# Half-width transposes for q and k, and a rearranged first batch, in an attention kernel followed by a token-mixing block

## The chip, the core and the metric

The kernel runs on one core of a Trainium2 chip. Five engines run their own instruction lists: TensorE (PE; its weight loads are shown as PEld), VectorE (DVE), ScalarE (ACT), GpSimd (POOL) and SyncE (SP). They wait for each other by semaphores. The metric is the device time of one execution in microseconds; the kernel before has a median of 174.81 us over 10 runs (174.43 to 175.35).

## The reference

Four batches, 8 heads, 768 tokens, head size 64. Attention with 8 global keys, a causal window of 96 and a bias that falls linearly with distance; then a token-mixing block on the 512 channels:

```python
scores = scale * q @ k^T
keep   = (key < 8) | (0 <= query - key < 96)
dist   = where(global and not local, 96, |query - key|)
a      = softmax(where(keep, scores - slope[h] * dist, -1e9))
x      = (a @ v) as (batch, 768, 512)
theta  = x @ w_theta
y      = w_tok_r @ (x * cos(theta)) + w_tok_i @ (x * sin(theta))
u      = x + y
out    = u + max(u @ w_ch, 0)
```

## The kernel before

The 768 tokens make 6 tiles of 128, the 8 heads make 4 pairs. A tile of keys meets only its own tile of queries, the next one, and the 8 global keys, so the scores of a pair are 11 blocks of 128x128 for each head, in three chunks of 4, 4 and 3 (`score_mms`, L279). The two heads of a pair lie on 64 partitions each, and their score matmuls use the upper and the lower half of TensorE's rows (form 64*128 in the profile). ACT takes the exponential of a chunk (`score_exp`, L298). In batch 0 the bias is added beforehand by a matmul of a diagonal matrix with the distances (`score_bias`, L270, on `diag` and `dist`); in the other batches the exponential is multiplied by a table `etab` (L312, L315), which `bias_table` (L140) makes on ACT. `values` (L336) multiplies by v, with a column of ones for the row sums, and DVE divides (L360, L362). `xtrans` (L364) turns the result into `xT`: by TensorE and a copy in batch 0, by DMA otherwise. Then `theta` (L378), cosine and sine on ACT (L395), products on DVE (L398), `mix` (L403), `utrans` (L418), `chan` (L430).

For the scores q and k must lie with the head size on the partitions. They are loaded with tokens on the partitions. Batch 0, pair 0 comes as float32 in `qk32` by SP and ACT (L99); the other loads convert to bf16 and are issued by POOL (L73, L82). DVE (for pair 0, DVE and ACT) copies a pair so that the two heads of a token tile are 128 adjacent columns: `qkn`, in `cast0` (L193) for batch 0 and in `prep_copy` (L224) for batches 1 and 2. Then one transpose for each token tile, 6 for q and 6 for k (L204, L244), writes a tile in PSUM, which DVE and ACT copy to `qT` and `kT` (L211, L249, L251). `kglob` (L214) copies four key blocks to `kG` and puts the global keys over their first 8 columns. Batch 3 is turned by DMA (`prep_dma`, L256) and has no `qkn`.

Order of the work: batch 0 up to `theta` and the tables is written out by hand (L510 to L574); each engine's list is kept in that order. After that a scheduler places the instructions, guided by the order of the program and by anchors (`behind`). `weave` (L488) mixes two lists of steps by their weights: the main one, token mixing of batch b, and the side one, the preparations and the attention of batch b + 1. `prep` of batch 1 is in the side list of batch 0, beginning when 0.3 of the main weight is done; `prep` of batch 2 is in that list too, among the attention of batch 1. The buffers of q and k serve two batches: batch 3 is loaded where batch 1 was, so its loads (L82) wait until that is read. PSUM is handed out as two double-width tiles (`ps_big`) and four single ones (`ps_small`), in rotation.

By hand, batch 0 is a loop over pairs. Each turn of the loop takes the exponentials, copies out the next pair's transposes, does the values of the pair before, and casts the pair after next; that pair's transposes are issued after the next pair's second chunk of scores. The last pair's values follow the loop (L566), then the first weight transposes, `xtrans` of the last pair, and `theta`.

Of the kernel before, what the change touches and what calls it, by code (L numbers as in the profile page):

```python
# [9 lines left out]
FP = mybir.dt.float32  # L10
BF = mybir.dt.bfloat16
AF = mybir.ActivationFunctionType
# [4 lines left out]
def kernel(  # L17
# [13 lines left out]
    nc = tc.nc  # L31
    B, H, S, D = q.shape
    T = 128
    NT = S // T
    DM = H * D
    NC = DM // T
    NP = H // 2
    NG = int(n_global)
    NL = int(n_local)
    W = T + NL  # L40
    scale = 1.0 / math.sqrt(D)
    slopes = [2.0 ** (-8.0 * (h + 1) / H) for h in range(H)]
# [91 lines left out]
    def diagonals(p):  # L134
        for h in (2 * p, 2 * p + 1):
            nc.vector.tensor_scalar(diag[:, h], ident, -slopes[h] / scale, None, op0=ALU.mult)

    etab = const.tile([T, H, 5, T], BF)

    def bias_table(p):  # L140
        for h in (2 * p, 2 * p + 1):
            nc.scalar.activation(etab[:, h], dist[:, 0:5], AF.Exp, scale=-slopes[h])

    halfpi = const.tile([T, 1], FP)
    junk = const.tile([T, 1], FP)
# [41 lines left out]
    def behind(eng):  # L187

        return tc.issue_after(anchor[eng]) if eng in anchor else nullcontext()

    tiles0 = {}

    def cast0(p, i_, eng, h=None):  # L193
        if (p, "n") not in tiles0:
            tiles0[p, "n"] = att.tile([T, NT, 2, 2, D], BF, name="qkn", bufs=2)
        src = qk32[:, i_] if p == 0 else loads[0][0][:, i_, 2 * p:2 * p + 2]
        hs = slice(0, 2) if h is None else slice(h, h + 1)
        eng(out=tiles0[p, "n"][:, :, i_, hs].rearrange("p t h d -> p h t d"), in_=src[:, hs])

    def turn0(p, i_):  # L200
        qkn = tiles0[p, "n"]
        ps = tiles0[p, i_] = ps_small([T, NT, T], BF)
        for t_ in range(NT):
            nc.tensor.transpose(ps[:, t_, :], qkn[:, t_, i_].rearrange("p h d -> p (h d)"), ident)  # L204

    def out0(p, i_, copy, half=None):
        to = qkT.setdefault((0, p), [None, None, None])
        if to[i_] is None:
            to[i_] = att.tile([T, S], BF, name=("qT", "kT")[i_], tag=("qT", "kT")[i_], bufs=6)
        ns = slice(0, T) if half is None else slice(half * T // 2, (half + 1) * T // 2)  # L210
        copy(out=to[i_].rearrange("p (n t) -> p n t", t=NT)[:, ns],  # L211
             in_=tiles0[p, i_].rearrange("p t n -> p n t")[:, ns])

    def kglob(b, p):  # L214
        kT = qkT[(b, p)][1]
        kG = qkT[(b, p)][2] = att.tile([T, NT - 2, T], BF, name="kG", bufs=6)
        with behind("dve") if b == B - 1 else nullcontext():
            nc.vector.tensor_copy(
                out=kG, in_=kT[:, T:(NT - 1) * T].rearrange("p (t n) -> p t n", t=NT - 2))
            nc.vector.tensor_copy(out=kG[:, :, 0:NG], in_=kT[:, None, 0:NG].to_broadcast([T, NT - 2, NG]))  # L220

    qkns = {}

    def prep_copy(b, p):  # L224
        qk = loads[b][0]
        qkn = qkns[b, p] = att.tile([T, NT, 2, 2, D], BF, name="qkn", bufs=2)
        with behind("dve"):
            for i_ in range(2):
                nc.vector.tensor_copy(
                    out=qkn[:, :, i_].rearrange("p t h d -> p h t d"), in_=qk[:, i_, 2 * p:2 * p + 2])  # L230

    def prep(b, p):
        if p == 0:
            prep_copy(b, 0)
        if p + 1 < NP:
            prep_copy(b, p + 1)
        qkn = qkns[b, p]
        qT = att.tile([T, S], BF, name="qT", bufs=6)
        kT = att.tile([T, S], BF, name="kT", bufs=6)
        for i_, dst in ((0, qT), (1, kT)):  # L240
            ps = ps_small([T, NT, T], BF)
            with behind("pe"):
                for t_ in range(NT):
                    nc.tensor.transpose(ps[:, t_, :], qkn[:, t_, i_].rearrange("p h d -> p (h d)"), ident)  # L244

            dst = dst.rearrange("p (n t) -> p n t", t=NT)
            src = ps.rearrange("p t n -> p n t")
            if i_ == 0:
                nc.vector.tensor_copy(out=dst, in_=src)  # L249
            else:  # L250
                nc.scalar.copy(out=dst, in_=src)  # L251

        qkT[(b, p)] = [qT, kT, None]
        kglob(b, p)
# [15 lines left out]
    def score_bias(p, c):  # L270
        pb = pbs[0, p, c] = ps_big()
        n = min(4, 2 * NT - 1 - 4 * c)
        s0 = 2 if c else 0
        for hh in range(2):
            nc.tensor.matmul(pb[:, hh, 0:n * T], lhsT=diag[:, 2 * p + hh],
                             rhs=dist[:, s0:s0 + n].rearrange("p s n -> p (s n)"),
                             start=True, stop=False)
# [55 lines left out]
            nc.vector.tensor_copy(out=vG[:, hs], in_=vn[:, hs, 1:NT - 1, :])  # L333
        nc.vector.tensor_copy(out=vG[0:NG, hs], in_=vn[0:NG, hs, 0:1, :].to_broadcast([NG, n, NT - 2, D + 1]))

    def values(b, p, hh):  # L336
        vn = loads[b][1]
        e_t, vG = ebuf[(b, p)], vGs[b]
        h = 2 * p + hh
        if b == 0:  # L340
            po = ps_small([T, 1, 512], FP)
        else:
            if hh == 0:
                pos[(b, p)] = ps_big()
            po = pos[(b, p)][:, hh:hh + 1, :]
        for it in range(NT):
            mms = [(e_t[:, hh, it, 0, :], vn[:, h, it, :])]
            if it:
                mms.append((e_t[:, hh, it - 1, 1, :], vG[:, h, it - 2, :] if it > 1 else vn[:, h, 0, :]))
            o = po[:, 0, it * (D + 1):(it + 1) * (D + 1)]  # L350
            for i_, (l_, r_) in enumerate(mms):
                nc.tensor.matmul(o, lhsT=l_, rhs=r_, start=(i_ == 0), stop=(i_ == len(mms) - 1))  # L352
        if b and hh == 0:
            return
        if b:
            po = pos[(b, p)]
        h0, n = (hh, 1) if b == 0 else (0, 2)
        po4 = po[:, :, 0:NT * (D + 1)].rearrange("p a (t d) -> p a t d", d=D + 1)
        rec = att.tile([T, n, NT, 1], FP, name="rec", tag=f"rec{n}")
        nc.vector.reciprocal(rec, po4[:, :, :, D:D + 1])  # L360
        xv = x_sb[b][:, p, :, h0 * D:(h0 + n) * D].rearrange("p t (a d) -> p a t d", a=n)
        nc.vector.tensor_mul(xv, po4[:, :, :, 0:D], rec.to_broadcast([T, n, NT, D]))  # L362

    def xtrans(b, p, copy=nc.vector.tensor_copy):  # L364
        if b:
            anchor["sp"] = nc.sync.dma_start_transpose(
                out=xT_sb[b][:, p, :].rearrange("p (t s) -> p t s", t=NT),
                in_=x_sb[b][:, p].rearrange("p t d -> p (t d)")).ins
            return
        ps = ps_small([T, S], BF)  # L370
        for st in range(NT):
            nc.tensor.transpose(ps[:, st * T:(st + 1) * T], x_sb[b][:, p, st, :], ident)
        copy(out=xT_sb[b][:, p, :], in_=ps)


    zri, u_sb, uTs, pss, css = {}, {}, {}, {}, {}
# [133 lines left out]
    warm(6)  # L510
    distances()
    diagonals(0)
    cast0(0, 1, dve, 0)
    cast0(0, 1, act, 1)
    turn0(0, 1)
    cast0(0, 0, dve, 0)
    cast0(0, 0, act, 1)
    turn0(0, 0)
    out0(0, 1, act, 0)
    out0(0, 1, dve, 1)  # L520
    out0(0, 0, act, 1)
    out0(0, 0, dve, 0)
    kglob(0, 0)
    score_bias(0, 0)
    score_bias(0, 1)
    score_mms(0, 0, 0)
    score_mms(0, 0, 1)
    score_exp(0, 0, 0)
    cast0(1, 1, dve)
    cast0(1, 0, dve)  # L530
    diagonals(1)
    turn0(1, 1)
    turn0(1, 0)
    for p in range(NP):
        nxt = p + 1 < NP
        score_exp(0, p, 1)
        if nxt:
            out0(p + 1, 1, act)
            out0(p + 1, 0, dve)
            kglob(0, p + 1)  # L540
        if p:
            values(0, p - 1, 0)
            values(0, p - 1, 1)
        score_bias(p, 2)
        score_mms(0, p, 2)
        score_exp(0, p, 2)
        if p + 2 < NP:
            cast0(p + 2, 1, dve)
            cast0(p + 2, 0, dve)
            diagonals(p + 2)  # L550
        if p == 0:
            vglob(0, 0, 4)
        if p == 1:
            vglob(0, 4, 4)
        if nxt:
            score_bias(p + 1, 0)
            score_mms(0, p + 1, 0)
            score_exp(0, p + 1, 0)
            score_bias(p + 1, 1)
            score_mms(0, p + 1, 1)  # L560
            if p + 2 < NP:
                turn0(p + 2, 1)
                turn0(p + 2, 0)
        if p:
            xtrans(0, p - 1, act if p == NP - 1 else dve)
    values(0, NP - 1, 0)  # L566
    values(0, NP - 1, 1)
    trans_w(0, nc.scalar.copy)
    xtrans(0, NP - 1)
    for c in range(NT // 2):  # L570
        theta(0, c, 0)
        theta(0, c, 1)
    for p in range(NP):
        bias_table(p)  # L574
    manual.close()
    for eng in (mybir.EngineType.PE, mybir.EngineType.DVE, mybir.EngineType.Activation):
        last = [i for i in nc.cur_bb.bb.instructions if i.engine == eng][-1]
# [82 lines left out]
```

The softmax here doesn't subtract the row's maximum and nothing guards it: scores larger than these inputs give would overflow.

## Time and profile before

| what | us |
|---|---|
| median of 10 runs | 174.81 |
| the profiled execution | 175.47 |
| its span, first to last instruction | 173.5 |
| PE, DVE, ACT busy in it | 161.0, 128.0, 99.2 |
| copies to `qkn`, batches 1 and 2 (L229, 16) | 5.1 |
| casts to `qkn`, batch 0, pairs 1 to 3 (L198 on DVE, 6) | 2.3 |
| transposes of q and k (L244 96, L204 48), PE busy | 7.6 and 4.0 |
| first exponential starts | 9.32 |
| first `theta` matmul of batch 0 | 27.49 |

How to read it: busy time of an engine is the union of its instructions' times. A matmul is shown with its whole passage (0.22 us for 128 columns), while the next can start long before it ends, so the distance between starts tells what PE spends on one. In a timeline row the first number is the start, the second the length, "x6" says that so many instructions were merged, and what stands in brackets is the idle time before it and what ended it. The granted TensorE clock was 0.996 of full speed.

### The profile page before, as it was taken

How to read it: one execution, taken by the hardware profiler on the slowest of the kernel's cores; microseconds unless marked ns; L12 is line 12 of the kernel's file. 1: busy time of each engine (PE TensorE's matmuls, PEld its weight loads, DVE VectorE, ACT ScalarE, POOL GpSimd, SP SyncE). 2: the span in 40 equal slices, each digit the busy share in tenths (PEclk: the TensorE clock that was granted, in tenths of full speed). 3: DMA queues.
4: the chain of work that ended last, by engine and by line, in shares of the span. 5: the costliest groups of instructions: out<-in, count | busy, mean ns of one | idle time of the engine just before them, and what ended most of it. 6: DMA issues, size and time to landing. Idle time of an engine off the chain costs nothing.

```text
span 173.5 us, 3652 instructions
## 1 busy us (share of the span) xinstructions
PE 161.0 (93%) x1482; PEld 84.3 (49%) x1482; DVE 128.0 (74%) x288; ACT 99.2 (57%) x124; POOL 37.4 (22%) x45
## 2 busy tenths in 40 slices
PE   6689989997999999999999998999999989999991
PEld 1445564453756466544454463444454634444440
DVE  7579964876999999999587588596786837723443
ACT  2489686997587695489834550879347308500010
POOL 8974347004182010099100000000000000000000
PEclk9999999999999999999999999999999999999998
DMA  4999999999999999799999697688137471413335
GB/s 153 186 194 179 210 211 205 205 204 168 164 204 171 162 154 160 95 112 158 211 133 125 156 137 165 140 154 237 31 76 117 122 168 36 155 36 101 105 93 181
DMA packets 75088, 25.92 MB, mean 149 GB/s; under 512 B 63168, under 2 KB 72128, under 8 KB 75072
## 3 DMA queue, kind: packets, MB, share of 16 engines
q0 software_dynamic: 45680, 12.45, 79.0%
q1 hardware_dynamic: 28976, 12.72, 35.0%
q10 hardware_dynamic: 416, 0.52, 0.9%
q8 instruction: 11, 0.18, 0.4%
q14 instruction: 5, 0.04, 0.1%
HBM read 25.69 MB, written 6.29 MB: 184 GB/s over the span
## 4 chain that ended last, share of the span: by engine, by line
PE 50%; DMA 33%; DVE 7%; POOL 5%; issue 1%; ACT 1%; SPq 0%; DVEq 0%; POOLq 0%
PE ps L409 26%; DMA qk<-in_k_dram 11%; PE ps L434 10%; DMA w_nat<-in_moe_w_tok_r_dram 8%; DMA xT<-x_sb 7%; DMA uT<-u 5%; PE pb L295 4%; PE pb L389 3%; PE pb L352 3%; POOL qk L73 3%; PE ps L389 2%; POOL vn L88 2%; DMA kT<-qk 2%; DVE qT L249 1%; DVE zri L398 1%
## 5 line engine op out<-in xcount | busy, mean ns | idle before, releaser
L409 PE MATMUL ps<-zri,w_tokT 128*128 128x512 bf16 x288 | 70.6, 380 | 0.3 <-DVE o_sb L440 0.2
L302 ACT ACTIVATE e<-pb 128x1024 bf16<-128x1024 f32 (+1 forms) x48 | 43.6, 958 | 22.3 <-PE pb L295 22.1
L409 PEld LDWEIGHTS <-w_tokT 128*128 128x128 bf16 x288 | 26.1, 98 | 28.9 <-issue 1.0
L414 DVE TENSOR_TENSOR u<-x_sb,ps 128x512 bf16<-128x512 bf16 x24 | 16.4, 682 | 14.6 <-PE ps L409 14.6
L434 PE MATMUL ps<-w_ch_bf,uT 128*128 128x512 bf16 x96 | 24.2, 380 | 0.4 <-DMA uT<-u 0.4
L398 DVE TENSOR_TENSOR zri<-x_sb,cs 128x512 bf16<-128x512 bf16 x48 | 17.9, 418 | 7.8 <-ACT cs L395 7.5
L440 DVE SCALAR_TENSOR_TENSOR o_sb<-ps,u 128x512 f32<-128x512 f32 (+1 forms) x25 | 16.5, 663 | 3.3 <-PE ps L434 3.3
L395 ACT ACTIVATE cs<-pb,halfpi 128x1024 bf16<-128x1024 f32 x8 | 8.9, 1115 | 15.6 <-PE pb L389 15.6
L312 DVE TENSOR_TENSOR e<-e,etab 128x1024 bf16<-128x1024 bf16 (+1 forms) x24 | 14.7, 615 | 3.7 <-ACT e L302 3.7
L389 PE MATMUL pb<-w_theta_bf,xT 128*128 128x512 bf16 x64 | 15.1, 380 | 1.2 <-DMA xT<-x_sb 1.2
L295 PE MATMUL pb<-qT,kT 64*128 64x128 bf16 x224 | 15.6, 219 | 0.2
L295 PEld LDWEIGHTS <-kT 64*128 64x128 bf16 x224 | 8.9, 94 | 14.1 <-issue 12.9
L389 PEld LDWEIGHTS <-xT 128*128 128x128 bf16 x96 | 9.1, 98 | 12.2 <-DMA xT<-x_sb 2.4
L428 ACT COPY uT<-ps 128x512 bf16<-128x512 bf16 x7 | 4.1, 587 | 18.8 <-PE ps L427 18.8
L352 PEld LDWEIGHTS <-e 128*128 128x128 bf16 x352 | 12.7, 97 | 3.1 <-issue 1.2
L434 PEld LDWEIGHTS <-uT 128*128 128x128 bf16 x96 | 8.8, 98 | 10.5 <-DMA uT<-u 0.9
L88 POOL DMA_DIRECT2D vn<-in_v_dram x5 | 9.6, 1930 | 11.0 <-PE ps L168 9.4
L295 PE MATMUL pb<-qT,kG 64*128 64x128 bf16 x128 | 11.7, 216 | 0.3 <-DVE kG L220 0.2
L362 DVE TENSOR_TENSOR x_sb<-pb,rec 128x768 bf16<-128x768 f32 x12 | 11.4, 948 | 0.3
L315 DVE TENSOR_TENSOR e<-e,etab 128x1024 bf16<-128x1024 bf16 x12 | 8.2, 684 | 2.8 <-ACT e L302 2.8
L251 ACT COPY kT<-ps 128x768 bf16<-128x768 bf16 x8 | 6.4, 799 | 5.9 <-PE ps L244 5.9
L352 PE MATMUL pb<-vn,e 128*128 128x65 bf16 x168 | 9.6, 193 | 0.1
(74 smaller groups left out, 205.2 us busy)
## 6 DMA issues: line engine op xcount, KB each, us to landing
out_dram<-o_sb SPq DMA_DIRECT2D x23, 256.0 KB, 2.4
vn<-in_v_dram POOLq DMA_DIRECT2D x3, 768.0 KB, 23.0
qk<-in_q_dram POOLq DMA_DIRECT2D x2, 768.0 KB, 20.7
qk<-in_k_dram POOLq DMA_DIRECT2D x2, 768.0 KB, 23.1
w_nat<-in_moe_w_tok_r_dram POOLq DMA_DIRECT2D x3, 384.0 KB, 14.2
w_nat<-in_moe_w_tok_i_dram POOLq DMA_DIRECT2D x3, 384.0 KB, 15.5
vn<-in_v_dram POOLq DMA_DIRECT2D x2, 384.0 KB, 9.3
qk<-in_q_dram POOLq DMA_DIRECT2D x8, 96.0 KB, 9.4
```

The lines of the kernel that those rows point to most:

```text
L88: nc.gpsimd.dma_start(out=vn[:, h0:h0 + n, :, 0:D].rearrange("p h t d -> p (h t) d"), in_=v[b, h0:h0 + n].rearrange("h (t p) d -> p (h t) ...
L295: nc.tensor.matmul(pb[:, hh, o:o + T], lhsT=lhsT, rhs=qT[R, (own, nxt)[part]], start=bool(b), stop=bool(b) or (jt == NT - 1 or (j == 1 and ...
L302: ins = nc.scalar.activation(e_c, pb[:, :, 0:n], AF.Exp, scale=scale).ins
L312: nc.vector.tensor_mul(e_c, e_c, tab[:, :, s0:s0 + n // T].rearrange("p a s n -> p a (s n)"))
L352: nc.tensor.matmul(o, lhsT=l_, rhs=r_, start=(i_ == 0), stop=(i_ == len(mms) - 1))
L362: nc.vector.tensor_mul(xv, po4[:, :, :, 0:D], rec.to_broadcast([T, n, NT, D]))
L389: nc.tensor.matmul(pb[j_] if last else pb[:, j_, :], lhsT=xT[:, dc, st(j_)], rhs=w_theta_bf[:, dc, :], start=(dc == 0), stop=(dc == NC - 1))
L398: nc.vector.tensor_mul(zri[b][:, i_, 2 * c + j_, :].rearrange("p (g d) -> p g d", g=NP), xb[:, :, 2 * c + j_, :], cs[:, i_, j_].rearrange( ...
L409: anchor["pe"] = nc.tensor.matmul(ps, lhsT=w_tokT[wi][:, st, tt * T:(tt + 1) * T], rhs=zri[b][:, wi, st, :], start=(st == 0 and wi == 0), ...
L414: anchor["dve"] = nc.vector.tensor_add(u_sb[b, tt].rearrange("p (g d) -> p g d", g=NP), x_sb[b][:, :, tt, :], ps.rearrange("p (g d) -> p g ...
L434: nc.tensor.matmul(ps_c, lhsT=uT[:, dc, :], rhs=w_ch_bf[:, dc, :], start=(dc == 0), stop=(dc == NC - 1))
L440: nc.vector.scalar_tensor_tensor(o_sb[:, cols], in0=ps_c[:, cols], scalar=0.0, in1=u[:, cols], op0=ALU.max, op1=ALU.add)
```

## The change

Transposes: the copies to `qkn` go, but for pair 0 of batch 0, whose float32 is cast to a bf16 tile `qk0` in the order in which it came. `turn` transposes each head of each token tile by itself: 64 columns in, 64 partitions out, at partition 0 or 64 of the same PSUM tile. A pair takes 24 of these instead of 12. This holds for batches 0, 1 and 2.

Batch 0 by hand: the first two score biases come before the casts, tables 0 and 1 are made early on ACT, the diagonals are made earlier on DVE. The first pair's `kglob` copies block 0 first and the other three after. Pair 1's transposes come between the first and the second chunk of pair 0's scores; those of pairs 2 and 3 come before the next pair's biases. The last pair's values, division, `xtrans` and the first `theta` are cut in token tiles 0 to 3 and 4 to 5; the copy of pair 2's `xT` moves from ACT to DVE.

```diff
-    def bias_table(p):
-        for h in (2 * p, 2 * p + 1):
-            nc.scalar.activation(etab[:, h], dist[:, 0:5], AF.Exp, scale=-slopes[h])
+    def bias_table(h):
+        nc.scalar.activation(etab[:, h], dist[:, 0:5], AF.Exp, scale=-slopes[h])
...
+    qk0 = att.tile([T, 2, 2, NT, D], BF, name="qk0", bufs=1)
+
+    def cast0(i_, eng, h):
+        eng(out=qk0[:, i_, h], in_=qk32[:, i_, h])
+
+    def turn(ps, src):
+        for t_ in range(NT):
+            for hh in range(2):
+                nc.tensor.transpose(ps[hh * D:(hh + 1) * D, t_, :], src[:, hh, t_, :], ident)
 
     def turn0(p, i_):
-        qkn = tiles0[p, "n"]
         ps = tiles0[p, i_] = ps_small([T, NT, T], BF)
-        for t_ in range(NT):
-            nc.tensor.transpose(ps[:, t_, :], qkn[:, t_, i_].rearrange("p h d -> p (h d)"), ident)
+        turn(ps, loads[0][0][:, i_, 2 * p:2 * p + 2] if p else qk0[:, i_])
...
-    def kglob(b, p):
+    def kglob(b, p, t0=0, t1=NT - 2):
         kT = qkT[(b, p)][1]
-        kG = qkT[(b, p)][2] = att.tile([T, NT - 2, T], BF, name="kG", bufs=6)
+        if t0 == 0:
+            qkT[(b, p)][2] = att.tile([T, NT - 2, T], BF, name="kG", bufs=6)
+        kG = qkT[(b, p)][2][:, t0:t1]
...
     def prep(b, p):
-        if p == 0:
-            prep_copy(b, 0)
-        if p + 1 < NP:
-            prep_copy(b, p + 1)
-        qkn = qkns[b, p]
+        qk = loads[b][0]
...
             with behind("pe"):
-                for t_ in range(NT):
-                    nc.tensor.transpose(ps[:, t_, :], qkn[:, t_, i_].rearrange("p h d -> p (h d)"), ident)
-
+                turn(ps, qk[:, i_, 2 * p:2 * p + 2])
...
-    def values(b, p, hh):
+    def values(b, p, hh, i0=0, i1=NT):
...
-        for it in range(NT):
+        for it in range(i0, i1):
...
-    def xtrans(b, p, copy=nc.vector.tensor_copy):
+    def xtrans(b, p, copy=nc.vector.tensor_copy, i0=0, i1=NT):
...
-        copy(out=xT_sb[b][:, p, :], in_=ps)
+        copy(out=xT_sb[b][:, p, own], in_=ps[:, own])
...
     diagonals(0)
-    cast0(0, 1, dve, 0)
-    cast0(0, 1, act, 1)
+    score_bias(0, 0)
+    score_bias(0, 1)
+    cast0(1, dve, 0)
+    bias_table(0)
+    cast0(1, act, 1)
     turn0(0, 1)
-    cast0(0, 0, dve, 0)
-    cast0(0, 0, act, 1)
+    cast0(0, dve, 0)
+    cast0(0, act, 1)
     turn0(0, 0)
+    diagonals(1)
     out0(0, 1, act, 0)
     out0(0, 1, dve, 1)
     out0(0, 0, act, 1)
     out0(0, 0, dve, 0)
-    kglob(0, 0)
-    score_bias(0, 0)
-    score_bias(0, 1)
+    kglob(0, 0, 0, 1)
     score_mms(0, 0, 0)
-    score_mms(0, 0, 1)
+    bias_table(1)
     score_exp(0, 0, 0)
-    cast0(1, 1, dve)
-    cast0(1, 0, dve)
-    diagonals(1)
+    kglob(0, 0, 1)
     turn0(1, 1)
     turn0(1, 0)
-    for p in range(NP):
-        nxt = p + 1 < NP
+    score_mms(0, 0, 1)
+    diagonals(2)
+    diagonals(3)
+    for p in range(NP - 1):
         score_exp(0, p, 1)
...
         score_exp(0, p, 2)
         if p + 2 < NP:
-            cast0(p + 2, 1, dve)
-            cast0(p + 2, 0, dve)
-            diagonals(p + 2)
...
+            turn0(p + 2, 1)
+            turn0(p + 2, 0)
...
-    values(0, NP - 1, 0)
-    values(0, NP - 1, 1)
-    trans_w(0, nc.scalar.copy)
-    xtrans(0, NP - 1)
-    for c in range(NT // 2):
+    p = NP - 1
+    score_exp(0, p, 1)
+    values(0, p - 1, 0)
+    values(0, p - 1, 1)
+    score_bias(p, 2)
+    score_mms(0, p, 2)
+    score_exp(0, p, 2)
+    values(0, p, 0, 0, 4)
+    values(0, p, 1, 0, 4)
+    xtrans(0, p - 1)
+    trans_w(0, act)
+    xtrans(0, p, dve, 0, 4)
+    theta(0, 0, 0)
+    values(0, p, 0, 4, 6)
+    values(0, p, 1, 4, 6)
+    theta(0, 0, 1)
+    xtrans(0, p, dve, 4, 6)
+    for c in range(1, NT // 2):
         theta(0, c, 0)
         theta(0, c, 1)
-    for p in range(NP):
-        bias_table(p)
+    for h in range(2, H):
+        bias_table(h)
```

## The prediction

> **What bounds the kernel now.** I first read part 2 of the page, the span in forty slices of 4.34 us, for which engines and which queue are full when.
>
> ```profile
> PE   6689989997999999999999998999999989999991
> DVE  7579964876999999999587588596786837723443
> DMA  4999999999999999799999697688137471413335
> ```
>
> TensorE (PE) is full from slice 9 to the end. VectorE (DVE) is full only from slice 10 to 18, while batches 1 and 2 are prepared. The DMA engines are full from slice 1 on, so up to about 65 us a load lands when the queue gets to it. The table of windows cuts out the stretch with the prepared batches.
>
> ```profile
> core 0: us, PE busy (x) PEld busy (x) DVE busy (x) ACT busy (x) POOL busy (x), PEclk, DMA share, GB/s
> 41.30:43.00 1.70, 0.74 (x11) 0.57 (x12) 0.68 (x3) 1.09 (x2) 0.00 (x0) 1.00 2.59 157
> 43.00:52.00 9.00, 8.85 (x102) 5.63 (x99) 9.00 (x23) 6.20 (x9) 4.31 (x6) 1.00 2.13 182
> 52.00:60.00 8.00, 7.82 (x113) 4.55 (x113) 8.00 (x17) 5.78 (x8) 1.42 (x2) 1.00 2.81 159
> 60.00:67.30 7.30, 6.86 (x112) 4.79 (x112) 7.30 (x17) 5.71 (x8) 0.83 (x1) 1.00 1.90 146
> ```
>
> From 43 to 67.3 us PE and DVE are both busy nearly always: 23.5 and 24.3 of 24.3 us. PE's hole is before it, at 41.3 to 43. The timeline of PE and DVE around it, and the chain of waits, say why.
>
> ```profile
> 41.27 0.51 PE L244 MATMUL ps<-ident,qkn 128*128 128x128 bf16 x6
> 42.32 0.90 DVE L229 COPY qkn<-qk 128x768 bf16<-128x768 bf16 x3 [1.11 <-DMA qk<-in_k_dram]
> 42.74 0.51 PE L244 MATMUL ps<-ident,qkn 128*128 128x128 bf16 x6 [0.96 <-DVE qkn L229]
> ...
> 22.89 19.41 DMA qk<-in_k_dram
> ```
>
> PE turns q of batch 1, then stands for 0.96 us: k of batch 1 lands at 42.30, issued at 22.89 and 19.41 us under way behind other loads, and DVE copies it until about 42.7. So time won before 41 us becomes a longer stand here, unless other PE work is put ahead of it.
>
> **Part 1, the transposes of batches 1 and 2 (8 pairs).** Removed: 16 DVE copies. Added: a turn of 12 half-width transposes in place of 6 whole ones, 16 times. The rows, grouped by form:
>
> ```profile
> L229 DVE COPY qkn<-qk 128x768 bf16<-128x768 bf16 x16 | 5.1, 345 | 1.1 <-DMA qk<-in_k_dram 1.1
> L244 PE MATMUL ps<-ident,qkn 128*128 128x128 bf16 x96 | 7.6, 219 | 1.5 <-DVE qkn L229 1.3
> L295 PE MATMUL pb<-qT,kT 64*128 64x128 bf16 x224 | 15.6, 219 | 0.2
> L352 PEld LDWEIGHTS <-e 128*128 128x128 bf16 x352 | 12.7, 97 | 3.1 <-issue 1.2
> ```
>
> A burst of 12 whole transposes takes 0.83 us, the last one 0.22 of it, so each costs (0.83-0.22)/11 = 0.056 us of PE and a turn of 6 costs 0.34. Half-width transposes in array tiles of 128x64 are not in this trace. Lower bound: two such tiles overlap as the row tiles of the scores do, where two heads of 64 rows start together and pairs follow each 0.055 us; a turn stays at 0.34. Upper bound: they don't overlap, 12 x 0.056 = 0.67, 0.34 more a turn, 16 x 0.34 = 5.4 us. Below nothing is excluded, since the same 128 columns stream for each pair. A rule speaks against the change: the Trainium skill's TensorEngine Tiling (Array Packing), Restrictions, says that column tiling switches off the fast weight load. By TensorE: Matmul & The Clock Gate, LDWEIGHTS, a plain load takes columns/1.2 ns, an estimate of 53 ns for 64 columns. The trace has 22 loads of 128 columns within 0.76 us, at most 0.032 each, so it has the fast load. If two 53 ns loads run side by side they fit under a pair of 0.055; if one after the other a pair takes 0.107 and the turn 0.64, almost the upper bound. I take the lower bound, because the row tiles, the nearest row, start their pairs of loads within 0.01 us of each other.
>
> The array must also change its tiling around each burst. The timeline shows the price of it between mixing and scores:
>
> ```profile
> 82.22 2.12 PE L409 MATMUL ps<-zri,w_tokT 128*128 128x512 bf16 x9
> 84.27 0.23 PE L295 MATMUL pb<-qT,kT 64*128 64x128 bf16 x2
> 84.39 0.22 PE L295 MATMUL pb<-qT,kT 64*128 64x128 bf16 x2
> 84.54 0.61 PE L409 MATMUL ps<-zri,w_tokT 128*128 128x512 bf16 x2
> ```
>
> Nine mixing matmuls 0.2175 apart have streamed out at 84.18; the scores start at 84.27, 0.09 later. Back again: 84.39 + 0.055 against 84.54, 0.095. The Trainium skill has such a drain (TensorEngine Tiling, Key Properties), but no number. The 96 transposes of L244 lie in 12 bursts (41.27 and 42.74 as one). Nine stand between whole-array work (two changes each), one between scores and whole-array work (one more), two between scores (none more, since a change is already there on each side): 9 x 2 + 1 = 19 changes, 19 x 0.095 = 1.8 us. PE is full there, so it is on the path. Between nothing (a change of columns alone needs no drain) and 0.19 a change (3.6 us), I take the row's 0.095.
>
> What comes back on PE: at 42.74 the turn of k starts when k lands, -0.40. At 59.92 and 61.52 PE stands 0.27 and 0.39 for a DVE copy, past the streaming of the work before; both go, -0.66. The other holes of PE between 43 and 74, worked out the same way (start less the end of streaming, less a change), sum to about 1.3 us; DVE, which some of them wait for, loses 5.1 of some 31 us. I credit a quarter, -0.33. The 5.1 us of DVE are otherwise hidden behind PE. Sum of part 1: 1.8 - 0.40 - 0.66 - 0.33 = **+0.4 us**.
>
> The waits move too. PE, in order, now waits itself for k; the 3 mixing matmuls (43.08) and the later turns stand behind it, as they do now. On POOL, the loads of batch 3's q and k (first issue 46.89, released by the last copy of a pair of batch 1) now wait for PE's last turn, which ends at 48.8: about 1.9 us later, with seven like them and v of batch 3 behind. The queue still holds q, k and v of batch 2 then (k of batch 2 lands near 55), so the engines don't run dry, and the first reader of batch 3's q and k is a DMA transpose at 97. Nothing. If the queue were dry it would still cost nothing. On SP nothing is moved.
>
> **Part 2, batch 0 (up to 32.7 us).** The biases ahead of data: four matmuls that took 1.77 us at 6.92 (0.43 apart) now start when DVE has dist and diag, about 4.4, and end at 6.1, while the first turn started at 5.66: 0.5 late. They no longer stand before the scores (0.4 won), and the key copy of one block instead of four shortens 0.64 us: the first exponential stays near 9.3. A bias table on ACT (0.64 us, dist to cast) pushes the cast at 5.09 by 0.1 at most; the second lies in ACT's idle 1.69 us before 9.32. The early diagonals on DVE (0.19 each) lie before 7.03, where DVE waits, or where the casts were. Six casts of pairs 1 to 3 go (2.3 us of DVE). Pair 1's turns now stand before the second score group: about +0.4 for ACT. Turning pairs 2 and 3 sooner frees PE for the scores at 20.07, before which ACT idled 1.19: -0.9. The last pair in two pieces: values of tiles 0 to 3 need no last exponential, so theta starts about 26.2, not 27.49, but pauses for the second piece; its 24 matmuls end near 31.8, not 32.67: -0.85. Together 0.4 - 0.9 - 0.85 = -1.35 us by 32.7 (five changes of tiling more, 0.5 us, fall mostly into waits of PE for DVE and ACT). I credit **nothing** of it, for PE then stands 1.35 us longer for k at 42.30. The two tables fewer at 36.8 (1.3 us of ACT) free ACT before 41.9, when only a copy read at 50.58 waits for it: nothing.
>
> **Sum.** The profiled execution took 175.47 us, span 173.5 and 1.97 around it; it becomes 173.9 and 175.87. That execution is 0.66 above the median of 174.81; the same +0.4 on the median gives **175.2**.
>
> **Rivals.**
> - *The gate is open* (not slower). The scheduler puts mixing of batch 0 ahead of k's turn, or the load lands sooner, so PE doesn't stand at 42.3. For it: L409, L168 and L427 work of batch 0 is left then. Against it: PE takes its list in order, and now it stands idle with that work in the list behind. It decides when the stand before k's first turn stays under 1 us although batch 0 ends over 1 us sooner; 0.4 - 1.35 on the median gives 173.9.
> - *Half-width transposes don't overlap.* For it: the missing fast load. Against it: the row tiles. 16 x 0.34 = 5.4 more: 180.6. A turn then takes 0.64 or more.
> - *The main case with other sizes*: changes free, -1.8 to give 173.4 at the extreme; changes at double price 177.0; likelier within 174.3 to 176.4, its own range.
>
> **How the numbers follow.** Main case 0.50, gate open 0.24, no overlap 0.26. About 0.2% (0.35 us) is what a measurement of this kernel can tell from no change. Of the main case 0.28 is slower, 0.16 within it, 0.06 faster. Faster 0.24 + 0.06 = 0.30; same 0.16; slower 0.28 + 0.26 = 0.54. The range goes from 173.3, under the open gate, to 180.6, the middle of the case without overlap; that leaves out 0.13 above and about 0.05 below.
>
> **What would show it.** In the changed profile: rows of form 128*64 in pairs 0.055 apart and turns of 0.34 (else no overlap); holes of about 0.095 on both sides of a burst; theta of batch 0 ending near 31.8; then a stand of over 2 us for k near 42.3. I am wrong if that stand is short, if the turn takes 0.6, or if DVE, no longer full, lets the holes of PE between 43 and 74 close altogether.

## The result, and the profile after

| | kernel before | changed kernel |
|---|---|---|
| median, us (lowest to highest, runs) | 174.88 (174.31 to 176.29, 49) | 176.88 (175.97 to 179.11, 14) |
| ratio, 95% interval | | 1.011 [1.0089, 1.013] |
| profiled execution, us; its span | 175.47; 173.5 | 178.16; 175.7 |

The changed kernel is 2.0 us slower by the medians; the ratio leaves out its one slow execution (179.11 us). Its profiled execution lies 1.3 us above its median, so a second one was profiled (176.33 us, span 174.2, called "after again" below). Where one number decides, both are given.

The slices of the changed kernel, from part 2 of its page, and the same windows as in the prediction:

```profile
PE   6569999999999999999996998999999979999991
DVE  7664976875999999867666577596786836733443
DMA  5999999999999999999999777789135371413334
```

```profile
core 0: us, PE busy (x) PEld busy (x) DVE busy (x) ACT busy (x) POOL busy (x), PEclk, DMA share, GB/s
41.30:43.00 1.70, 1.34 (x18) 0.67 (x16) 0.96 (x1) 0.75 (x1) 0.00 (x0) 1.00 2.47 158
43.00:52.00 9.00, 8.51 (x145) 5.46 (x144) 8.79 (x20) 6.61 (x10) 4.68 (x5) 1.00 2.13 183
52.00:60.00 8.00, 7.59 (x132) 4.96 (x127) 7.94 (x15) 5.07 (x7) 1.86 (x3) 1.00 2.09 177
60.00:67.30 7.30, 7.11 (x115) 4.68 (x113) 7.08 (x15) 5.93 (x8) 0.83 (x1) 1.00 2.12 129
```

PE's hole before 43 us is half filled (1.34 of 1.70 us busy, 0.74 before). From 43 to 67.3 us PE and DVE are still nearly full. Nothing of 2 us is to be found there. The waits of PE for DMA are another matter. Two groups of the page, first of the kernel before, then of the changed one (the last part of a row is PE's idle time before the group and what ended it):

```profile
L434 PE MATMUL ps<-w_ch_bf,uT 128*128 128x512 bf16 x96 | 24.2, 380 | 0.4 <-DMA uT<-u 0.4
...
L389 PE MATMUL pb<-w_theta_bf,xT 128*128 128x512 bf16 x64 | 15.1, 380 | 1.2 <-DMA xT<-x_sb 1.2
```

```profile
L422 PE MATMUL ps<-w_ch_bf,uT 128*128 128x512 bf16 x96 | 24.2, 380 | 1.6 <-DMA uT<-u 1.6
...
L377 PE MATMUL pb<-w_theta_bf,xT 128*128 128x512 bf16 x64 | 15.4, 380 | 1.8 <-DMA xT<-x_sb 1.8
```

Waits for `uT` and `xT`, tiles that DMA transposes write and that the diff doesn't touch, grew from 1.6 to 3.4 us. The chain of waits (start, length, what) shows which transposes; the same two transfers before and after:

```profile
84.91 9.35 DMA uT<-u
...
139.47 2.75 DMA xT<-x_sb
```

```profile
85.25 10.54 DMA uT<-u
...
141.02 3.36 DMA xT<-x_sb
```

They took 1.19 and 0.61 us longer. Against the kernel before, the span is 2.15 us longer: 0.34 of it is there when batch 1's mixing begins, 1.19 comes between that and batch 1's `chan`, 0.61 in the last batch's `theta`, 0.01 elsewhere. "After again" has -0.17, 0.41 and 0.42. These are single executions. By the medians of all runs the span grew from 172.9 us (65 runs) to 174.3, so 1.4 us of the loss lies in it. The time outside the span was 1.9 to 2.2 us before; it is mostly 2.1 to 2.3 in the changed kernel, and 2.5 to 3.7 in 4 of its 14 runs.

Why should these transposes take longer? SyncE's timeline shows it for the second, before and after:

```profile
136.85 1.21 SPq L366 DMA_TRANSPOSE xT<-x_sb  x1
138.16 1.22 SPq L423 DMA_TRANSPOSE uT<-u  x1
139.47 1.24 SPq L366 DMA_TRANSPOSE xT<-x_sb  x1
```

```profile
138.40 1.21 SPq L353 DMA_TRANSPOSE xT<-x_sb  x1
139.71 1.22 SPq L411 DMA_TRANSPOSE uT<-u  x1
141.02 1.81 SPq L353 DMA_TRANSPOSE xT<-x_sb  x1
```

SyncE's command for the third took 1.81 us instead of 1.24. The DMA view of the changed kernel, cut to 140.6 to 141.2 us, has one foreign packet in it:

```profile
q8 instruction: 1, 0.02, 10.7%
```

The same view of the kernel before, 139.0 to 141.0 us, has none on this queue. Within the span q8 carries 11 packets of 16,384 bytes before and 12 after; between two of them the trace records 205 to 288 TensorE instructions after 97 us, 134 to 358 earlier. I read them as TensorE's own program, fetched block by block, and call each one a fetch. The Trainium skill (Runtime: NRT & Kernel Launch, Instruction fetch mechanics) says that an engine fetches blocks of 256 instructions through a DMA queue of its own while it runs, and that crossing into a new block is mostly hidden. The size agrees. What a fetch does to the other transfers the section doesn't say, and that is the question here. The change adds 288 TensorE instructions (2964 to 3252 by the pages, weight loads counted), so every block after batch 0 is fetched at another moment.

### The profile page after: what moved, and what is told of

Same layout as the page of the kernel before. It is cut to its first block, busy times and chain, and to the rows that moved or that the text cites. A ratio compares the mean times of both kernels' runs of the same rounds, so it can differ in the third digit from the quotient of the medians.

```text
span 175.7 us, 3921 instructions
## 1 busy us (share of the span) xinstructions
PE 161.0 (92%) x1626; PEld 83.5 (48%) x1626; DVE 124.4 (71%) x274; ACT 98.5 (56%) x123; POOL 38.4 (22%) x45
## 3 DMA queue, kind: packets, MB, share of 16 engines
q0 software_dynamic: 45680, 12.45, 75.1%
## 4 chain that ended last, share of the span: by engine, by line
PE 47%; DMA 32%; DVE 12%; POOL 5%; issue 1%; ACT 1%; SPq 0%; DVEq 0%; POOLq 0%
PE ps L397 25%; DMA qk<-in_k_dram 11%; PE ps L422 9%; DMA w_nat<-in_moe_w_tok_r_dram 7%; DMA xT<-x_sb 7%; DMA uT<-u 6%; PE pb L281 4%; PE pb L377 3%; PE pb L338 3%; POOL qk L73 3%; PE ps L377 2%; DVE e L298 2%; POOL vn L88 2%; DMA kT<-qk 2%; DVE qT L235 2%; DVE o_sb L428 1%
## 5 line engine op out<-in xcount | busy, mean ns | idle before, releaser
L281 PE MATMUL pb<-qT,kT 64*128 64x128 bf16 x224 | 15.0, 219 | 2.1 <-DVE qT L211 1.2
L281 PEld LDWEIGHTS <-kT 64*128 64x128 bf16 x224 | 8.8, 94 | 15.1 <-issue 13.5
L200 PE MATMUL ps<-ident,qk 128*64 128x128 bf16 x288 | 11.3, 222 | 2.1 <-DMA qk<-in_k_dram 1.8
L200 PEld LDWEIGHTS <-qk 128*64 128x64 bf16 x288 | 8.9, 109 | 5.9 <-issue 2.5
```

Source lines behind the costliest of these rows:

```text
L200: nc.tensor.transpose(ps[hh * D:(hh + 1) * D, t_, :], src[:, hh, t_, :], ident)
L281: nc.tensor.matmul(pb[:, hh, o:o + T], lhsT=lhsT, rhs=qT[R, (own, nxt)[part]], start=bool(b), stop=bool(b) or (jt == NT - 1 or (j == 1 and ...
```

## The experiments

**Theory (fetches):** the new transposes themselves cost next to nothing; their number moves the instruction fetches, and a fetch that meets a DMA transpose, or the tail of the loads, holds it up. **Rival 1:** the loss is the added TensorE work and its changes of tiling. **Rival 2:** the new timing of the first 70 us (waits, loads, order) is the loss. The first four runs take the change apart and were made before the theory of the fetches; it was read out of their traces.

**Batch 0's part alone** (batches 1 and 2 by copies and whole transposes, as before):

```diff
...
-                turn(ps, qk[:, i_, 2 * p:2 * p + 2])
+                for t_ in range(NT):
+                    nc.tensor.transpose(ps[:, t_, :], qkn[:, t_, i_].rearrange("p h d -> p (h d)"), ident)
```

> The changed kernel with whole transposes and the copies to qkn back in batches 1 and 2; batch 0 stays rearranged and half-width. Tiling theory (the changes of TensorE's tiling in batches 1 and 2 are the cost, batch 0 is worth nothing): near the kernel before, 174.5 to 175.2 us. Batch-0 theory (the rearranged first batch costs, by where it leaves the later DMA waits): it stays near 176.9, at least 176.3. Wait theory (both halves are near nothing and the loss is a longer DMA wait near 95 us that any change of order can set off): anywhere from 174.5 to 177, told by the hole ahead of the channel matmuls near 95 us, 0.6 us before and 1.8 us in the changed kernel.

Measured 175.57 us, beside 175.06 for the kernel before: 1.0029 [1.0002, 1.0056]. That is a little above the range of the tiling theory and under that of the batch-0 theory; the range of the wait theory holds it, but is wide. PE has no wait for `uT` near 95 us in its profile.

**Batches 1 and 2 alone** (the kernel before with `turn` in `prep`):

> The kernel before with half-width transposes straight from the loaded q and k in batches 1 and 2 only; batch 0 as before. Tiling theory: 176.3 to 177 us, all of the loss. Batch-0 theory: 174.4 to 175.2, no loss. Wait theory: by the hole near 95 us. In each case the turn of 12 half-width transposes should take 0.31 us of distance between starts and two changes of tiling of 0.095 stand around each burst.

Measured 175.14: 1.0011 [0.9995, 1.0028]. So this part, the one I costed at +0.4 us, costs between -0.1 and 0.5 us, and the whole change costs more (1.1%) than the two parts together (0.3% and 0.1%). This speaks against the tiling theory (176.3 to 177 expected) and against rival 1, in which the costs would add up. In the second kernel PE waits 1.0 us for `xT` and not at all for `uT`, though it has all the half-width turns of batches 1 and 2:

```profile
L423 PE MATMUL ps<-w_ch_bf,uT 128*128 128x512 bf16 x96 | 24.2, 380 | 0.0
...
L378 PE MATMUL pb<-w_theta_bf,xT 128*128 128x512 bf16 x64 | 14.8, 379 | 1.0 <-DMA xT<-x_sb 1.0
```

**Turns of pairs 2 and 3 late again** (in the changed kernel, after the next pair's second chunk of scores, as before):

```diff
-        if p + 2 < NP:
-            turn0(p + 2, 1)
-            turn0(p + 2, 0)
...
+        if p + 2 < NP:
+            turn0(p + 2, 1)
+            turn0(p + 2, 0)
```

> The changed kernel with the transposes of pairs 2 and 3 of batch 0 back after the next pair's second chunk of scores, where the kernel before has them. In the changed kernel TensorE stands 1.5 us at 12.5 us for the load of pair 2's k, and ACT with it. Here that stand should go and the first theta matmul come 1 us sooner. Theory that time won before 41 us is lost again at the load of batch 1's k: 176.5 to 177 us, with the stand before the first turn of k longer by about as much. Rival, that the front carries through: 175.6 to 176.1.

Measured 176.73: 1.0089 [1.0054, 1.0125]. The stand of PE at 12.49 us (its line is in the next section) is gone, but `theta` of batch 0 starts only 0.15 us sooner (26.88 instead of 27.03), not 1 us. PE then stands 0.98 us for k of batch 1 instead of 0.36, and the time stays that of the changed kernel, as the theory had it. As the front hardly moved, this tests the theory only weakly.

**`uT` of batch 1's first two tiles by TensorE** (in the changed kernel):

```diff
-        if b and (b, tt) != (B - 1, NT - 1):
+        if b and (b, tt) != (B - 1, NT - 1) and (b, tt) not in ((1, 0), (1, 1)):
```

> The changed kernel with the first two u tiles of batch 1 turned by TensorE and copied by ACT, as batch 0's are, in place of the DMA transposes that TensorE waits for near 95 us (1.8 us of hole in the changed kernel, 0.6 in the one before). Costs 8 transposes (0.45 us of TensorE). Wait theory: 175.3 to 175.9 us, the hole is gone and what lies behind moves up. Tiling theory: little, 176.4 to 177, since another wait or the work itself takes its place.

Measured 177.94: 1.0152 [1.0121, 1.0183], slower still; expected were 175.3 to 175.9, or 176.4 to 177. PE doesn't wait for that transfer any more. It does the 8 transposes (0.45 us, as expected) and waits 0.51 us for DVE ahead of the first of them:

```profile
84.89 0.40 PE L415 MATMUL ps<-ident,u 128*128 128x128 bf16 x4 [0.51 <-DVE u L402]
```

Until batch 1's `chan` its profile shows no other wait of PE of more than 0.1 us. So what took the place of the transfer is the edit's own work, 1.3 us with the changes of tiling around it; that this run's median lies above the changed kernel's is not explained by it.

The next four add TensorE instructions without meaning: the first transpose of a turn of batch 0 is done several times into the same place. What is computed stays the same.

**The changed kernel with 50 more transposes:**

```diff
-        turn(ps, loads[0][0][:, i_, 2 * p:2 * p + 2] if p else qk0[:, i_])
+        turn(ps, loads[0][0][:, i_, 2 * p:2 * p + 2] if p else qk0[:, i_]); [nc.tensor.transpose(ps[0:D, 0, :], loads[0][0][:, i_, 2 * p, 0, :], ident) for _ in range([0, 1, 12, 12][p])]
```

> The changed kernel with the first half-width transpose of a turn of batch 0 done again (12 times in each turn of pairs 2 and 3, once in those of pair 1): 50 more transposes, 100 more TensorE instructions, same results, nothing else moved. They lie before 35 us, where the exps set the pace. Theory (fetches): [...] a fetch stretches a DMA transpose of SP that starts within half a us of it; 100 more instructions put the fetches near 85.9, 93.1, 108.3, 126.3, 136.5 and 160.2 us, clear of the transposes at 100.75 and 141.02, and the last one comes before the last store. Then no transpose after 97 us takes over 1.3 us, the hole for xT in the last theta is back to about 0.6 us from 1.24, the part outside the span to 2.1 us, and the median falls by 0.6 to 1.5 us, to 175.4 to 176.3. Rival (the change's own TensorE work, changes of tiling or the order of its waits is the loss): more TensorE work can't help; 176.9 or more.

Measured 177.23: 1.0131 [1.0113, 1.0149]. The theory's time was missed, and the rival's was met. The repeats were not in the shadow: batch 1's mixing begins at 82.14 instead of 81.05. From there to the end, though, it takes 92.65 us instead of 94.62, and 93.65 in "after again": in the last batch's `theta` the theory came true (the wait for `xT` is 0.48 us and the transpose is not stretched), and was paid for in front. One other transpose after 97 us was still stretched, to 1.67 us.

**The changed kernel with 24 more transposes** (6 in each turn of pairs 2 and 3):

> As the one with 50, but 24 more transposes (6 in each turn of pairs 2 and 3), 48 more instructions: a control. Theory (fetches): they fall near 88.6, 98.0, 114.6, 129.0, 138.8 and 165.8 us, onto the close chain of DMA transposes on SP of 98 to 117 us twice and near the one of 138.4; one or two transposes of 1.6 us or more remain, the last block comes inside the span; 176.2 to 177.0. Rival (TensorE work or order): 176.9 or a little more, between the changed kernel and the one with 50.

Measured 176.79: 1.0112 [1.0076, 1.0149], with a wide spread (175.80 to 178.32): in the theory's range, and too near the rival's to decide. Its profile is of the fastest run. The fetches fell at 83.5, 93.9, 108.8, 125.0, 136.8 and 161.2 us, up to 6 us from where I had put them: counting instructions doesn't say to a us when a block is fetched.

**The kernel before with 14 more transposes:**

```diff
-        for t_ in range(NT):
+        for t_ in [0] * [0, 1, 3, 3][p] + list(range(NT)):
```

> The kernel before with 14 of batch 0's full-width transposes done again (3 in each turn of pairs 2 and 3, 1 in those of pair 1), 28 more TensorE instructions. Theory (fetches): near 90.8, 98.5, 116.4, 130.0 and 139.5 us, so that the xT transpose of 139.47 is stretched to about 1.8 us as in the changed kernel, the one of 99.84 perhaps no longer: theta of the last batch takes 0.5 us longer; 175.0 to 175.8. Rival (what the change adds is the loss): 0.8 us of early TensorE work in the shadow of the exps changes nothing: 174.8 to 175.1.

Measured 177.74: 1.0144 [1.0116, 1.0172]. This run says most. Fourteen transposes, some 0.8 us of TensorE before 35 us, and nothing of the change: and the kernel is as slow as the changed one. Both expectations are missed, the rival's (174.8 to 175.1) and the theory's (175.0 to 175.8). Of the 2.13 us that its span is longer than the kernel before's, 0.74 is in the last batch's `theta`, where the theory put 0.5; 0.52 is there when batch 1's mixing begins, and 0.87 comes between that and `chan`. The added instructions explain why its fetches fall where the changed kernel's do: 288 are one block of 256 and 32 more, and 14 transposes with their weight loads are 28. Its fetches come at 90.8, 100.3, 118.1, 130.5 and 140.8 us; those of the changed kernel at 90.4, 100.4, 118.0, 130.2 and 140.7. Its chain of waits and SyncE's timeline show the same two places:

```profile
85.43 10.22 DMA uT<-u
...
140.88 3.49 DMA xT<-x_sb
```

```profile
139.57 1.22 SPq L423 DMA_TRANSPOSE uT<-u  x1
140.88 1.92 SPq L366 DMA_TRANSPOSE xT<-x_sb  x1
```

and its page has the changed kernel's waits and more:

```profile
L434 PE MATMUL ps<-w_ch_bf,uT 128*128 128x512 bf16 x96 | 24.2, 380 | 1.3 <-DMA uT<-u 1.3
...
L389 PE MATMUL pb<-w_theta_bf,xT 128*128 128x512 bf16 x64 | 15.5, 380 | 2.6 <-DMA xT<-x_sb 2.6
```

**The kernel before with 62 more transposes** (3 in each turn of pair 1, 14 in each of pairs 2 and 3):

> The kernel before with 62 of batch 0's transposes done again (14 in each turn of pairs 2 and 3, 3 in those of pair 1), 124 more TensorE instructions. Theory (fetches): near 86.1, 92.5, 106.6, 126.1 and 135.1 us, clear of the uT transpose of 99.84 us that took 2.12 us: the chain of transposes on SP up to 116 us is 0.9 us shorter; if that chain sets the mix of batch 2, 174.0 to 174.6, else 174.9. Rival (TensorE work counts): 3.4 us more of it before 35 us, up to 1 us of it visible: 175.0 to 176.0.

Measured 177.51: 1.0155 [1.0134, 1.0175]; expected were 174.0 to 174.6, a miss. Batch 0's `theta` starts at 30.49 instead of 27.49, too late to be hidden: batch 1's mixing begins 1.7 us late (82.43). After that it takes 92.85 us, the kernel before 92.81: four times the useless transposes of the run above, and none of its loss in the second half.

The last four test these readings.

**The changed kernel with 12 more transposes** (3 in each turn of pairs 2 and 3):

> The changed kernel with 12 half-width transposes of batch 0 done again (3 in each turn of pairs 2 and 3), 24 more TensorE instructions. Theory (fetches): the same kind of addition that cost the kernel before 1.4% should here gain, since it takes the fetches off the transposes: near 139.1 us instead of 140.7, between the transposes of 138.40 and 139.71, near 100.0 instead of 100.4, and the last block at 168 us, before the last store. The xT transposes of the last batch take 1.2 us each and the hole in its theta is 0.6 us; 175.6 to 176.4, if the fetch falls there (it has wandered by up to 1 us). Rival (every added TensorE instruction or every delay before 35 us costs): 177.0 to 178.

Measured 176.23: 1.0102 [1.0066, 1.0138], beside the changed kernel's 177.05 (1.0136 [1.0097, 1.0175]). Of the direction that the theory asks for, and in its range, but the intervals overlap. The profile is of the fastest run; in it the fetch came at 138.3 us (not 139.1) and still met the `xT` transpose, later in its course: that took 1.51 us instead of 1.81, not the 1.2 expected. PE no longer waits for `uT`:

```profile
L422 PE MATMUL ps<-w_ch_bf,uT 128*128 128x512 bf16 x92 | 23.8, 380 | 0.2
...
L377 PE MATMUL pb<-w_theta_bf,xT 128*128 128x512 bf16 x61 | 15.1, 380 | 1.4 <-DMA xT<-x_sb 1.2
```

**The kernel before with 4 more transposes** (1 in each turn of pairs 2 and 3):

> The kernel before with 4 of batch 0's transposes done again (1 in each turn of pairs 2 and 3), 8 more TensorE instructions. Theory (fetches): near 91.1, 98.8, 117.1, 130.4 and 142.3 us, about where they are in the kernel before, none on the transposes of the last batch; 174.8 to 175.3. Rival (any addition costs): 175.5 or more, part of what 14 cost.

Measured 174.95: 1.0009 [0.9984, 1.0033]. Not every addition costs. The fetches that matter here are where the kernel before has them (91.6, 99.2, 142.7 us), and so are its waits. Its `theta` of batch 0 starts at 28.32 us, as late as with 14 more (28.29; 27.49 before), so that delay alone is not what 14 more cost.

**The changed kernel once more:**

> The changed kernel unchanged, for a second profile: does its median of 176.9 hold, and are its waits of 95 us (hole of 1.79 us) and 141 us (xT transpose of 1.81 us) those of one execution or of the kernel? Theory (fetches): the fetch near 140.7 us and the stretched transpose beside it come again; the hole near 95 us may differ. Rival: a fresh profile shows neither, and the loss must be looked for elsewhere.

Measured 177.05: 1.0136 [1.0097, 1.0175]. Both places come again: the fetch at 139.4 with 1.64 us for the `xT` transpose of 139.73, and 9.76 us for `uT` from 84.74 on, with a fetch at 90.0. The wait for `uT` is shorter than in the first profile (0.8 us instead of 1.6).

**The kernel before, batch 0 later without a TensorE instruction more:**

```diff
...
-        score_exp(0, p, 2)
+        score_exp(0, p, 2); _ = p == NP - 1 and nc.scalar.copy(out=idle, in_=zero)
```

> The kernel before with one more copy of 128x512 zeros on ScalarE after batch 0's last exp: what comes after is about 0.5 us later, as with 14 more transposes, but no TensorE instruction is added. Theory (fetches): the fetches stay at the same instructions, so at the same transposes as in the kernel before; at most 0.5 us is seen, 174.9 to 175.4. Rival (a front that ends 0.5 us later meets the loads badly): as with 14 more transposes, 177 to 178.

Measured 174.54: 0.9986 [0.9964, 1.0008]. `theta` of batch 0 starts 0.48 us late (27.97) and batch 1's mixing doesn't (80.36). This speaks against rival 2, as far as half a us goes: a front that ends so much later costs nothing. Nor did one that ended sooner gain: with batch 0's part alone `theta` starts at 26.82, and batch 1's mixing at 80.65 (80.71 before).

All profiles together, worked out from their traces (us; "stretch A" is from batch 1's first mixing matmul to its first `chan`, "stretch B" from the last batch's first `theta` to its first mixing, "rest" from batch 1's first mixing to the end of the span):

| kernel | fetch between 82 and 97 | stretch A | fetch between 132 and 144 | stretch B | rest |
|---|---|---|---|---|---|
| before | 91.8 | 13.59 | 143.2 | 8.42 | 92.81 |
| before, 4 more | 91.6 | 13.42 | 142.7 | 8.45 | 92.66 |
| before, later | 92.0 | 13.96 | 143.8 | 8.44 | 93.20 |
| before, 62 more | 84.8, 96.2 | 13.24 | 138.1 | 8.42 | 92.85 |
| batch 0's part alone | 84.1, 94.1 | 13.00 | 136.1 | 8.43 | 92.91 |
| batches 1, 2 alone | 90.3 | 13.00 | 132.1 | 8.42 | 92.21 |
| after, 50 more | 82.3, 95.2 | 13.00 | 136.3 | 8.43 | 92.65 |
| after, 24 more | 83.5, 93.9 | 13.00 | 136.8 | 8.65 | 92.94 |
| after, 12 more | 85.0, 95.8 | 13.06 | 138.3 | 8.72 | 92.72 |
| **after** | 90.4 | 14.78 | 140.7 | 9.03 | 94.62 |
| **after again** | 90.0 | 14.00 | 139.4 | 8.84 | 93.65 |
| **after, turns late** | 90.0 | 13.75 | 139.6 | 8.86 | 93.44 |
| **before, 14 more** | 90.8 | 14.46 | 140.8 | 9.16 | 94.42 |
| **after, `uT` by TensorE** | 88.9 | 14.32 | 139.8 | 8.80 | 94.09 |

The five profiles in bold, of four kernels with and without the change, have a fetch at 88.9 to 90.8 and one at 139.4 to 140.8, which begins 0.1 to 0.4 us ahead of the last batch's `xT` transpose. They need 93.4 to 94.6 us for the rest, the others 92.2 to 93.2. The table was sorted so after the runs, and the two stretches do not say the same.

Stretch B follows the fetch closely. Undisturbed, the last batch's `xT` transpose takes 1.24 us and the stretch 8.42 to 8.45. Where a fetch meets it, it takes 1.51, 1.58, 1.64, 1.67, 1.81 and 1.92 us, and the stretch 8.72, 8.80, 8.84, 8.86, 9.03 and 9.16: the stretch grows by what the transpose grows, to within 0.06 us. (With 24 more the fetch meets the transpose before it: 1.43 and 8.65.) Over all 14 profiles, after 97 us, 336 DMA transposes that no fetch of TensorE overlapped took SyncE at most 1.33 us; of 54 that one overlapped 24 took 1.51 to 2.12. Which ones is a matter of the moment: of the 29 that started between 0.76 us ahead of the fetch's start and 0.51 us behind it, 24 were stretched, of the other 25 none.

Stretch A is another matter. It takes 13.0 us when PE waits for no `uT`; nearly all above that is the wait for this transfer (in the last row it is that edit's own work). In all 13 profiles in which this `uT` goes by DMA it lands within 0.62 us of v of batch 3, the last of the loads, and in twelve within 0.4, though it was issued 6 to 10.5 us before. The load of v, before and after:

```profile
L88 POOL DMA_DIRECT2D vn<-in_v_dram x1: 2269/2269/2269, 80.7 to 80.7; - x1
DMA to landing us min/median/max: 13.6/13.6/13.6
```

```profile
L88 POOL DMA_DIRECT2D vn<-in_v_dram x1: 2280/2280/2280, 81.2 to 81.2; - x1
DMA to landing us min/median/max: 14.9/14.9/14.9
```

So `uT` is late where that load is. The fetch near 90 us runs among its last packets (the fetch itself took 1.6 to 2.2 us in the bold rows, 0.9 to 1.4 elsewhere), but that it holds the load up is not shown: the kernel before with a later batch 0 has 13.96 without such a fetch, "after, turns late" 13.75 with it, and "batches 1, 2 alone" has one at 90.3 and no loss, as its loads were over at 89.9. Why v takes 14.9 us in "after" and with 14 more, and 13.5 to 14.0 in the five other profiles in which PE waits for `uT` (two of them with the change), is open.

## Why the prediction was right in its time and wrong in its reasons

The sign came out, and 176.9 lies in the range of 173.3 to 180.6, but above the main case's own 174.3 to 176.4. It is in the range by luck: that far up the range stands for changes of tiling at double price (177.0) or half-width transposes that don't overlap (180.6), and neither came true. Of the 2.0 us that were lost my sum had 0.4, and for another cause.

*Overlap of half-width transposes: right.* I took the lower bound, a turn that costs no more than before. From the first start to the last end a whole turn took 0.51 us, a half-width one takes 0.53. The rows of the changed kernel (the first two from its timeline, the third from its page):

```profile
40.80 0.53 PE L200 MATMUL ps<-ident,qk 128*64 128x128 bf16 x12
...
41.68 0.53 PE L200 MATMUL ps<-ident,qk 128*64 128x128 bf16 x12 [0.36 <-DMA qk<-in_k_dram]
```

```profile
L200 PEld LDWEIGHTS <-qk 128*64 128x64 bf16 x288 | 8.9, 109 | 5.9 <-issue 2.5
```

In the trace two start 4 ns apart and pairs follow each 0.056 us, as the row tiles do; the two weight loads of a pair start 3 ns apart. The weight load of 64 columns takes 109 ns, that of 128 columns 97 to 98: no faster for half the columns, which fits the Trainium skill's rule (TensorEngine Tiling (Array Packing), Restrictions) that column tiling loses the fast load, but the pairs stay 0.056 apart, so it stays hidden.

*Nineteen changes of tiling, 1.8 us: the price right, the balance wrong.* A change costs 0.09 to 0.10 us where nothing else is waited for, also one of columns alone (128x128 to 128x64, 0.092 to 0.094), for which I had thought of nothing as a lower bound. From 41.5 to 73.3 us 19 changes have a half-width turn on one side, as forecast. But those between scores and whole-array work fell from 26 to 15, so in all there are 34 instead of 26: 8 more, 0.75 us. The count was read off the order of before, which the scheduler doesn't have to keep.

*The gains in the same stretch, 0.40 + 0.66 + 0.33: too large.* PE's other holes there, worked out from the starts, fall from some 3.2 to some 2.5 us. That is about 0.7, and the changes eat it. Nothing remains of the +0.4, and "batches 1, 2 alone" (+0.1%, -0.05 to +0.28) agrees with either.

*Part 2, 1.35 us sooner by 32.7: wrong.* Batch 0's `theta` starts at 27.03 instead of 26.2, and its last matmul at 32.51 (32.46 before), so it ends near 32.7, not 31.8. The turn of pair 2, moved forward, now waits for its load, and ACT behind it; the timeline of the changed kernel:

```profile
12.49 0.86 PE L200 MATMUL ps<-ident,qk 128*64 128x128 bf16 x24 [1.45 <-DMA qk<-in_k_dram]
...
14.27 1.02 ACT L288 ACTIVATE e<-pb 128x1024 bf16<-128x1024 f32 x1 [1.51 <-PE pb L281]
```

The prediction had not asked when pair 2's keys land: at 12.45 us. Without the stand `theta` would start only 0.15 us sooner, as the run with late turns shows, because ACT then waits for scores later (1.19 us before 20.76). And the second piece comes late: its `xtrans` runs at 29.00, and `theta` pauses.

*Crediting it at nothing: not refuted, but for a wrong reason.* I expected a stand of over 2 us for k of batch 1. It is 0.36 us, and by my own test that step is wrong: the front gained too little, and k landed at 41.64 instead of 42.30. The chain of the changed kernel shows another place further on that can hide the front, a transposed `xT` that is 8.41 us under way and holds batch 1's `theta`:

```profile
64.91 8.41 DMA xT<-x_sb
73.36 3.20 PE pb L377 x14
```

Batch 1's mixing begins at 80.3 to 81.2 us in twelve of the 14 profiles, whether `theta` of batch 0 began at 26.8 or at 28.3 (82.1 and 82.4 with 50 and 62 more). That this `xT` is the reason was not tested.

*The failed step.* "The first reader of batch 3's q and k is a DMA transpose at 97. Nothing", and that the sum ended at 67 us. I asked who reads those loads, and not what else is under way with them: `uT` of batch 1 is, and lands when v of batch 3 lands. Nor did I ask what an added TensorE instruction does after its own moment: it shifts the fetches, and one falls on the last `xT` transpose. Mis-sized is not a term of the sum; a term was missing. In the two profiles of the changed kernel it measures 1.80 us (1.19 for `uT` and 0.61 for `xT`) and 0.83 us (0.41 and 0.42), out of spans that are 2.15 and 0.67 us longer than the kernel before's.

How far this is shown: that added instructions alone, without the change, bring a loss as large is shown (14 more), and that 8 instructions with as late a front, or half a us of delay alone, don't. For the last batch's `theta`, 0.4 to 0.6 us of the loss, the fetch is well tied to the stretched transpose, by the moment and by the length; still, no run could move a fetch and nothing else. For `uT` of batch 1, 0.4 to 1.2 us, the late load is shown and its cause is open. The time outside the span is open too. Over 2.3 us of it occur only in runs of the changed kernel, of the one with late turns and of the one before with 14 more, and these are the kernels whose trace has a block fetched after the last instruction (at 177.4 us in the changed kernel's first profile; its second shows none); that the fetch is the cause was not tested. None of the 12 runs was clearly faster than the kernel before.

## What to carry to other kernels

A change that only adds short instructions can cost where it has none: look in the profile for DMA waits that grew in places the diff doesn't touch, and lay the times of the instruction packets beside them. Before a loss or a gain of 1% is put down to an idea, shift the program by a few useless instructions in a place with slack: if the kernel before gets as slow, the idea is not what was measured. A gain in front is worth what the next join lets through; here 0.7 us sooner and 0.8 us later both went unseen (batch 0's part alone, 4 more).

## What the runs showed of the hardware that I had not expected

What I read as a block of TensorE's instructions (16,384 bytes on q8) occupies its DMA packet for 0.9 to 1.6 us, and for up to 2.2 us near 90 us, among loads. A DMA transpose of SyncE that starts from 0.76 us ahead of such a packet to 0.51 us behind its start took 1.5 to 2.1 us instead of 1.2, in 24 of 29 cases. Fourteen 128-column transposes, 0.8 us of TensorE in batch 0, made a kernel of 174.9 us 1.4% slower; 62 of them left its second half alone and cost only by their own length in front. Half-width transposes in pairs cost TensorE no more than whole ones, 0.056 us a pair, but for the change of tiling, 0.09 to 0.10 us. The moment of a fetch follows the instruction count only roughly: adding 48 instructions moved fetches by 4 to 9 us where the count alone gave 1 to 3.
